# Each token block stored as two transfers of 64 rows, with the orders of all engines written anew

## The chip, the cores and the metric

One core of a Trainium2 chip. The time is that of one execution on the device, in microseconds (us); of several runs the median is taken.

## The reference

The kernel computes a linear attention with the delta rule and a two-layer network behind it. With 4 batches, 8 heads, 768 tokens and a head size of 48:

```python
for t in range(S):                       # per batch and head
    y[t] = q[t] @ state
    v_old = k_n[t] @ state               # k_n: k of unit length
    state += beta[t] * outer(k_n[t], v[t] - v_old)
x = y as [4*768 tokens, 8*48 = 384]
h = x @ w_in                             # 384 -> 2048
out = gelu_tanh(h) @ w_out               # 2048 -> 384, float32
```

## The kernel before

The tokens are cut into 12 chunks of 64 (`C`). A chunk holds the 64 tokens of all four batches and eight heads. The 128 partitions are two halves of 64 tokens: half 0 holds batches 0 and 1, half 1 batches 2 and 3. A *unit* u is a chunk (u // 2) with every other head (u % 2); there are 24.

*Preparation of a unit* (`prep`): POOL or another engine makes normalized k (`kn`), k times beta (`kb`) and q in bf16 (`qb`) in the tile `tok`. These are turned, so that the head size lies on the partitions, into `kT`: for units 0 to 5 by TensorE (`T`), from unit 6 on by a transposing transfer that SP issues (`turn.u`). TensorE then makes the products of keys (`G2`, `G`), which DVE masks (`ln`, `wp`). Five steps of two products each (`A`, `B`, line 620) build the inverse of a triangular matrix; DVE adds to the results (`rt`), ACT and DVE copy them (`bde`, `xi`), and POOL copies and selects (`bdc`, `X1`). The lengths of k are `sq`, `sum`, `pow`, `eps`, `inv`.

*The chain of a chunk* (`chain`): from the state, `K`, `R`, `Um`, `Un`, `S`, `Sn` make the next state, and `Q`, `O` and the copy `On` give the attention's output in the tile `xo`. It is turned into `xT` by another transposing transfer on SP (`turnx`, line 742) for all chunks but the first and the last.

*The network of a chunk* (`mlp`): 256 tokens. `up` (line 775, three matmuls) makes 128 columns of h from `xT`, ACT applies `gelu`, and `down` (line 787) sums over the 2048. The 256 tokens are two *blocks* of 128 rows, b = 0 and b = 1. A block is copied from PSUM into one of four buffers `ob` by ACT or DVE (`Z`, line 381) and stored (line 798). Block 0 holds 64 tokens of batch 0 in partitions 0 to 63 and 64 of batch 2 in the others; block 1 those of batches 3 and 1. Block 0 leaves in one transfer with two runs of 64 rows (`outw`, 192 KB, 12 in all), block 1 in two transfers of 64 rows (`out`, 96 KB each, 24 in all). All are issued by SP but one of the last block, which ACT issues. The names carry a number: chunk c has blocks 2c+4 and 2c+4.5, so the last are 26 and 26.5.

*The order.* No compiler orders the work. The table `ORDER` lists, for each engine, every operation in the order in which that engine runs it; SP's list holds the transfers (loads of q, k and v, the turns, the stores). For an operation of ACT, DVE or POOL the list also settles which engine runs it. `BANKS` lists the PSUM bank of each product. From both, `schedule` and `emit` work out which semaphores each operation waits for. An engine runs its list in order: what stands behind a waiting operation waits too. `fill` are matmuls without use (line 433), that keep TensorE at work at the start.

Of the kernel before, what the change touches and what calls it, by code (L numbers as in the profile page):

```python
# [12 lines left out]
C = 64  # L13
# [13 lines left out]
        Xh.0.8/1 B.2/1 B.3/0 T.4/0 A.2/2 up.3.5/0 A.3/1 up.3.5/1 B.2/2 up.3.5/2 B.3/1 up.3.5/3 up.3/0 fill/61 up.3/1 fill/62 up.3/2
        A.3/2 S.0.5/0 up.3.25/0 up.3/3 G2.4/0 G.4/0 B.3/2 up.3.25/1 A16.2/0 up.3.25/2 fill/63 up.3.25/3 fill/64 A16.3/0 K.2.5/0 B.2/3
        A.4/0 B.3/3 down.4.5/0 up.3.75/0 fill/65 up.3.75/1 B.4/0 up.3.75/2 A32.2/0 A32.3/0 up.3.75/3 down.4.54/0 A.4/1 B.3/4 B.2/4
        down.4.58/0 B.4/1 T.5/0 down.4.62/0 Um.2.5/0 Q.2.6/0 G2.5/0 G.5/0 A.4/2 O.2.7/0 fill/66 fill/67 B.4/2 S.2.5/0 down.4/0 A.5/0  # L30
        down.4.04/0 down.4.08/0 B.5/0 A16.4/0 down.4.12/0 B.4/3 A.5/1 up.5.25/0 up.5.75/0 up.5.25/1 B.5/1 up.5.25/2 A32.4/0 up.5.75/1
        up.5.25/3 A.5/2 up.5.75/2 B.4/4 up.5.75/3 up.5/0 B.5/2 up.5/1 K.4.5/0 G2.6/0 up.5/2 up.5/3 up.5.5/0 A16.5/0 up.5.5/1 G.6/0
        B.5/3 up.5.5/2 G2.7/0 up.5.5/3 A.6/0 A32.5/0 G.8/0 G2.8/0 B.6/0 down.6.5/0 B.5/4 A.6/1 down.6.54/0 down.6.58/0 G.7/0
        down.6.62/0 Um.4.5/0 A.8/0 B.6/1 Q.4.6/0 G2.9/0 O.4.7/0 down.6/0 A.6/2 B.8/0 G.9/0 down.6.04/0 B.6/2 A.7/0 down.6.08/0 A.9/0
        B.7/0 A.8/1 A16.6/0 down.6.12/0 B.9/0 B.8/1 A.7/1 B.6/3 up.7.25/0 A.9/1 up.7.25/1 up.7/0 up.7.25/2 B.7/1 A32.6/0 A.8/2 B.9/1
        up.7.25/3 B.6/4 up.7/1 S.4.5/0 up.7/2 A.7/2 up.7.75/0 up.7/3 up.7.5/0 B.8/2 up.7.5/1 B.7/2 up.7.5/2 K.6.5/0 up.7.75/1 up.7.5/3
        A16.7/0 up.7.75/2 A.9/2 up.7.75/3 B.7/3 A16.8/0 down.8/0 B.9/2 A32.7/0 down.8.04/0 B.8/3 B.7/4 down.8.08/0 A16.9/0 down.8.12/0
        Um.6.5/0 A32.8/0 Q.6.6/0 G2.10/0 O.6.7/0 S.6.5/0 G.10/0 B.8/4 down.8.5/0 B.9/3 down.8.54/0 A.10/0 G2.11/0 K.8.5/0 G.11/0
        down.8.58/0 B.10/0 down.8.62/0 up.9.75/0 up.9.75/1 up.9.25/0 up.9.75/2 A32.9/0 up.9.75/3 A.10/1 up.9.25/1 B.9/4 up.9.25/2
        up.9.5/0 up.9.25/3 up.9.5/1 B.10/1 up.9.5/2 A.11/0 up.9.5/3 G2.13/0 G.13/0 Um.8.5/0 B.11/0 A.10/2 Q.8.6/0 G2.12/0 O.8.7/0  # L40
        G.12/0 A.13/0 B.10/2 up.9/0 B.13/0 up.9/1 A.11/1 up.9/2 A.12/0 up.9/3 A.13/1 B.11/1 B.12/0 S.8.5/0 down.10/0 A.12/1
        down.10.04/0 A16.10/0 B.13/1 A.11/2 up.11.75/0 B.12/1 up.11.75/1 B.10/3 B.11/2 down.10.08/0 up.11.75/2 A.13/2 up.11.75/3
        A16.11/0 down.10.12/0 up.11/0 B.13/2 up.11/1 A.12/2 A32.10/0 B.11/3 up.11/2 up.11.25/0 B.12/2 up.11.25/1 up.11/3 up.11.25/2
        B.10/4 A16.12/0 up.11.25/3 A32.11/0 up.11.5/0 K.10.5/0 up.11.5/1 B.11/4 down.10.5/0 up.11.5/2 A16.13/0 B.12/3 up.11.5/3
        down.10.54/0 B.13/3 Um.10.5/0 down.10.58/0 A32.12/0 Q.10.6/0 S.10.5/0 O.10.7/0 G.14/0 down.10.62/0 down.12.5/0 A32.13/0 B.12/4
        down.12.54/0 B.13/4 down.12.58/0 G2.14/0 K.12.5/0 down.12/0 down.12.62/0 down.12.04/0 G2.15/0 G.15/0 A.14/0 Um.12.5/0
        down.12.08/0 B.14/0 down.12.12/0 Q.12.6/0 G2.17/0 O.12.7/0 G.17/0 up.13.75/0 up.13.5/0 up.13.75/1 up.13/0 up.13.75/2 up.13/1
        up.13.75/3 up.13/2 A.15/0 up.13/3 A.14/1 up.13.5/1 G2.16/0 B.15/0 up.13.5/2 up.13.25/0 B.14/1 up.13.5/3 up.13.25/1 G.16/0
        S.12.5/0 up.13.25/2 up.15.5/0 up.13.25/3 up.15.5/1 A.16/0 up.15.5/2 A.17/0 up.15.5/3 A.15/1 A.14/2 B.16/0 down.14/0 B.17/0
        down.14.04/0 B.14/2 B.15/1 A.16/1 up.15/0 down.14.08/0 A.17/1 B.16/1 up.15/1 A.15/2 up.15/2 down.14.12/0 B.15/2 up.15.25/0  # L50
        B.17/1 A16.14/0 up.15.25/1 A.16/2 up.15/3 up.15.25/2 A16.15/0 up.15.25/3 B.14/3 A.17/2 B.15/3 K.14.5/0 B.16/2 up.15.75/0
        B.17/2 up.15.75/1 A32.14/0 up.15.75/2 up.15.75/3 A32.15/0 G.18/0 G2.18/0 B.14/4 B.15/4 down.14.5/0 A16.17/0 down.14.54/0
        A16.16/0 down.14.58/0 Um.14.5/0 B.16/3 A.18/0 down.14.62/0 S.14.5/0 Q.14.6/0 G2.19/0 down.16/0 B.17/3 down.16.04/0 G.19/0
        O.14.7/0 K.16.5/0 down.16.08/0 A32.16/0 B.18/0 A.19/0 down.16.12/0 A32.17/0 down.16.5/0 B.19/0 down.16.54/0 B.16/4 A.18/1
        A.19/1 down.16.58/0 G2.20/0 G.20/0 down.16.62/0 B.17/4 up.17.5/0 B.18/1 up.17.5/1 up.17.75/0 B.19/1 A.20/0 Um.16.5/0
        up.17.75/1 up.17.5/2 G2.21/0 up.17.5/3 B.20/0 up.17.75/2 up.17.25/0 up.17.75/3 A.20/1 up.17.25/1 A.19/2 up.17.25/2 up.17/0
        up.17.25/3 Q.16.6/0 G.21/0 O.16.7/0 up.17/1 B.19/2 up.17/2 B.20/1 up.17/3 A.18/2 S.16.5/0 A.21/0 A16.19/0 B.18/2 down.18/0
        B.21/0 down.18.04/0 A16.18/0 down.18.08/0 B.19/3 A.21/1 A.20/2 B.18/3 K.18.5/0 down.18.12/0 up.19.5/0 B.21/1 up.19.5/1 B.20/2
# [797 lines left out]
```

## Time and profile before

| | |
|---|---|
| Median of 3 runs | 276.76 us (274.14 to 276.99) |
| The profiled execution | 277.13 us |
| its span, first to last instruction | 275.4 us |
| mean granted clock of TensorE in it | 0.986 |
| busy: PE, DVE, ACT, POOL | 250.3, 203.7, 176.6, 143.3 us |
| DMA: packets, bytes | 118348, 32.06 MB |

The page gives for each engine how long it was busy; PE is TensorE, PEld its weight loads, SP issues transfers. In 40 equal slices of the span (6.9 us each) a digit tells the busy share in tenths. `PEclk` is the clock granted to TensorE, and `DMA` the mean busy share of the 16 DMA engines. A row of the waits tells which engine stood at which line, and what ended that. The chain of waits goes back from the last instruction, at each step to what released it. `SPq` is the issue of a transfer by SP; "to landing" counts from there until the data have arrived.

### The profile page before, as it was taken

To read this page: it belongs to the slowest core of one execution; us is meant where nothing else is said; L and a number is where in the kernel's file an instruction comes from. 1 tells how busy PE (TensorE), PEld (TensorE's weight loads), DVE (VectorE), ACT (ScalarE), POOL (GpSimd) and SP (SyncE) were. 2 spreads that over 40 slices of the span, in tenths; PEclk is the share of its full clock that TensorE was granted. 3 is DMA by queue.
4 is the path that set the end of the run, shared out by engine and by line. 5 is a ranking of instruction groups with operands and counts; after the bars stand their busy time and mean duration, and the time that the engine had idled before them with its cause. 6 is when DMAs were issued, how large, how long until landed. Compare 5 with 4: busy or idle time off the path is not lost.

```text
span 275.4 us, 12507 instructions
## 1 busy us (share of the span) xinstructions
PE 250.3 (91%) x5640; PEld 190.0 (69%) x5652; DVE 203.7 (74%) x336; ACT 176.6 (64%) x273; POOL 143.3 (52%) x221
## 2 busy tenths in 40 slices
...
PEclk9999999999999999799999999999999999999996
DMA  7999999699999699857969669749077500321031
GB/s 118 160 159 142 159 201 203 119 152 134 162 150 144 98 155 130 163 114 162 156 105 154 68 135 137 163 89 151 7 150 80 126 14 2 68 65 45 0 69 45
DMA packets 118348, 32.06 MB, mean 116 GB/s; under 512 B 112408, under 2 KB 117528, under 8 KB 118296
## 3 DMA queue, kind: packets, MB, share of 16 engines
...
q14 instruction: 8, 0.07, 0.1%
...
## 4 chain that ended last, share of the span: by engine, by line
PE 65%; DMA 16%; DVE 6%; POOL 3%; ACT 3%; issue 2%; SPq 1%; ACTq 0%; POOLq 0%; DVEq 0%
PE ps L787 19%; PE ps L775 18%; PE ps L620 14%; DMA kT<-tok 6%; DMA xT<-xo 5%; DMA qraw<-in_q_dram 3%; PE ps L433 2%; PE ps L592 2%; PE ps L665 2%; PE ps L544 1%; DMA braw<-in_beta_dram 1%; PE ps L552 1%; DVE wp L574 1%; PE ps L524 1%; PE ps L698 1%
## 5 line engine op out<-in xcount | busy, mean ns | idle before, releaser
L775 PE MATMUL ps<-xT,W 128*128 128x256 bf16 x576 | 84.3, 276 | 5.5 <-DMA xT<-xo 5.3
L381 ACT ACTIVATE bd<-ps 64x512 bf16<-64x512 f32 x114 | 66.5, 590 | 18.3 <-PE ps L620 16.3
L787 PE MATMUL ps<-W,gT 128*128 128x384 bf16 x384 | 75.6, 326 | 0.0
L780 ACT ACTIVATE gT<-ps 128x1024 bf16<-128x1024 f32 x48 | 48.4, 1020 | 31.5 <-PE ps L775 31.0
L775 PEld LDWEIGHTS ps<-xT,W 128*128 128x128 bf16 x576 | 49.1, 99 | 14.3 <-issue 5.4
L627 DVE TENSOR_TENSOR rt<-ps,two 128x512 bf16<-128x512 f32 x66 | 44.3, 686 | 11.3 <-PE ps L620 10.7
L614 POOL COPY bd<-xi 64x256 f32<-64x256 f32 x64 | 25.1, 395 | 40.6 <-ACT xi L381 28.3
L610 POOL TENSOR_SCALAR_AFFINE_SELECT bd<-ln 64x512 bf16<-64x512 bf16 x44 | 28.8, 656 | 29.5 <-DVE ln L559 25.5
L787 PEld LDWEIGHTS ps<-W,gT 128*128 128x128 bf16 x384 | 32.7, 97 | 15.9 <-ACT gT L780 0.2
L381 DVE CAST bd<-ps 64x512 bf16<-64x512 f32 x42 | 28.8, 687 | 5.4 <-PE ps L620 4.6
L627 DVE TENSOR_TENSOR rl<-ps,two 128x384 bf16<-128x384 f32 (+1 forms) x44 | 21.0, 484 | 11.3 <-PE ps L620 10.8
L574 DVE CAST_PREDICATED wp<-mup,ps 128x1024 bf16<-128x1024 uint16 x22 | 26.7, 1218 | 2.9 <-PE ps L544 2.8
L493 POOL TENSOR_TENSOR nrm<-nrm,half 128x16 f32<-128x16 f32 x9 | 26.7, 2965 | 0.2
L620 PE MATMUL ps<-rt,bd 128*128 128x64 bf16 x528 | 26.0, 193 | 0.6 <-DVE ln L559 0.5
L620 PE MATMUL ps<-wp,bd 128*128 128x64 bf16 (+1 forms) x528 | 24.8, 188 | 1.6 <-ACT bd L381 1.0
L620 PEld LDWEIGHTS ps<-rt,bd 128*128 128x128 bf16 x528 | 21.8, 98 | 5.3 <-DVE rt L627 1.7
L620 PEld LDWEIGHTS ps<-wp,bd 128*128 128x128 bf16 x528 | 21.1, 97 | 5.5 <-ACT bd L381 1.2
L381 ACT ACTIVATE xi<-ps 128x512 bf16<-128x512 f32 (+1 forms) x35 | 17.6, 516 | 10.2 <-PE ps L592 4.9
L516 POOL TENSOR_TENSOR tok<-tok,bsb 128x384 bf16<-128x384 bf16 x21 | 17.3, 831 | 10.8 <-PE ps L707 6.6
L514 POOL TENSOR_TENSOR tok<-kraw,nrm 128x384 bf16<-128x384 f32 x22 | 18.2, 833 | 6.5 <-DVE nrm L497 6.1
L559 DVE CAST_PREDICATED ln<-mlo,ps 128x512 bf16<-128x512 uint16 (+1 forms) x26 | 16.6, 643 | 4.5 <-PE ps L552 4.1
L433 PE MATMUL ps<-wz 128*128 128x512 bf16 x56 | 16.9, 418 | 2.1 <-DVE wz L387 1.2
...
## 6 DMA issues: line engine op xcount, KB each, us to landing
...
out_dram<-ob SPq DMA_DIRECT2D x23, 96.0 KB, 3.8
...
kraw<-in_k_dram SPq DMA_DIRECT2D x3, 96.0 KB, 3.6
```

The source lines that it names most:

```text
L381: return e.activation(out, in_, ACT.Copy) if e is nc.scalar else e.tensor_copy(out, in_)
L433: return e.matmul(P(f"fill{i}")[:, :], wz[:, 0:128], wz[:, 0:512])
L493: e.tensor_tensor(nr[:, 1, hx], nr[:, 0, hx], half[:, hx], ALU.pow),
L514: A("dve" if u < 2 else POOL, z + "kn", lambda e, P: e.tensor_tensor(kn, kr, nr[:, 3, hx].rearrange("t (p g) -> t p g", p=2).unsqueeze(3). ...
L574: A("dve", z + "wp", lambda e, P: e.copy_predicated(wp[s][:, :, :], mup[:, :].bitcast(U16).unsqueeze(1).to_broadcast([128, H, 2 * C]), P(p ...
L610: A("pool", z + "X1", lambda e, P, src=src, dst=dst: e.affine_select(out=dst, in_=src, compare_op=ALU.not_equal, fill=1.0, base=0, pattern ...
L614: A("pool", z + "bdc", lambda e, P, src=src, dst=dst: e.tensor_copy(dst.bitcast(F32), src.bitcast(F32)), reads=[w("xi")], writes=[n(f"bd{a ...
L620: ins = e.matmul(P(name)[:, C * h + lo:C * h + C], bd[s][:, h, :], rhs[:, h, lo:C])
L627: A("dve", z + f"rt{lo or str()}", lambda e, P, i=i, lo=lo, r_=r_: e.tensor_tensor(r_[:, :, lo:C], P(ps(f"A{i}")).rearrange("p (h t) -> p ...
L775: ins = e.matmul(P(ph)[:, w * f:w * f + w].rearrange("p (x t) -> p x t", x=2), W1[:, j, 128 * (i + f):128 * (i + f) + 128], x_[:, :, j, :] ...
L780: A("act", z + "gelu", lambda e, P, i=i, ph=ph: e.activation(g_[:, i:i + nf, 0:w], P(ph).rearrange("p (f t) -> p f t", f=nf), ACT.Gelu_app ...
L787: ins = e.matmul(P(po)[:, 0:DM], g_[:, f, 128 * b:128 * b + 128], W2[:, f, :], start=(f == 0), stop=(f == FC - 1))
```

## The change

In `mlp`, every block is stored in two transfers of 64 rows; the case of one transfer with two runs is gone. There are 48 transfers out instead of 36, of the same bytes. The lists of all five engines and the banks are written anew; of that part the diff shows one line.

```diff
-        loadk.-40/0 beta.-24.5/0 loadk.-40/3 loadk.-40/2 loadk.-39/0 loadk.-39/1 loadq.-40/1 loadq.-39/0 loadq.-40/0 loadq.-39/1
+        loadk.-40/1 beta.-24.5/1 beta.-24.5/0 loadk.-40/3 loadk.-39/0 loadk.-39/1 loadq.-39/1 loadq.-39/0 loadq.-40/0 loadq.-40/1
...
-                rows = out.rearrange("(a p c t) m -> p c a t m", a=2, p=2, t=C)[b % 2, g[b // 2]]
-                for a in (0, 1) if b % 2 else (slice(0, 2),):
-                    A("act" if final and a else "sp", z + "out" if b % 2 else z + "outw", lambda e, P, a=a, o_=o_, rows=rows, b=b: e.dma_start(
-                        rows[a ^ 1] if b % 2 else rows, o_[hf(a), :] if b % 2 else o_[:, :]),
+                for a in range(2):
+                    r0 = (2 * (a ^ b % 2) + b % 2) * S + C * g[b // 2]
+                    A("act" if final and a else "sp", z + "out", lambda e, P, a=a, r0=r0, o_=o_: e.dma_start(out[r0:r0 + C, :], o_[hf(a), :]),
                       reads=[f"ob{oi}"], dma=f"o{oi}" if not final else f"of{a}", pos=kz)
```

The order of the large pieces on PE (units, chains, ups and downs) is nearly the same; between them products change places, and there are 61 fillers instead of 68. On ACT and DVE, 29 of the copies `bde` go each way, 11 copies `xi` go from ACT to DVE and 7 back. Of the squares `sq`, four go from ACT to POOL and one comes back.

SP, around the turns of units 10 and 11 (`kT4`, `kT5`) and the turn of `xT` behind them (`xT3`, of chunk 3). `s0` to `s3` are the semaphores of PE, ACT, DVE and POOL. Before:

```order
L462 DMA kraw0<-in_k_dram 64x16x48
L798 DMA out_0_dram<-ob0 2x64x384
L462 DMA qraw0<-in_q_dram 64x16x48
L798 DMA out_0_dram<-ob2 2x64x384 [waits s2]
L527 DMA_TRANSPOSE kT4<-tok0 128x12x128 [waits s3]
L527 DMA_TRANSPOSE kT5<-tok0 128x12x128 [waits s3]
L462 DMA kraw1<-in_k_dram 64x16x48 x2
L462 DMA vraw2<-in_v_dram 64x16x48
L742 DMA_TRANSPOSE xT3<-xo1 128x6x128 [waits s1]
```

In the change:

```order
L797 DMA out_0_dram<-ob0 64x384 x2
L461 DMA qraw1<-in_q_dram 64x16x48
L461 DMA kraw0<-in_k_dram 64x16x48 x2
L461 DMA qraw2<-in_q_dram 64x16x48 [waits s3]
L526 DMA_TRANSPOSE kT4<-tok0 128x12x128 [waits s3]
L526 DMA_TRANSPOSE kT5<-tok0 128x12x128 [waits s3]
L797 DMA out_0_dram<-ob1 64x384
L461 DMA vraw2<-in_v_dram 64x16x48
L461 DMA vraw1<-in_v_dram 64x16x48
L461 DMA kraw1<-in_k_dram 64x16x48 [waits s3]
L741 DMA_TRANSPOSE xT3<-xo1 128x6x128 [waits s1]
```

Of the two stores with two runs ahead of the turns, one is now two halves; the other block (6) leaves later, and the wait for DVE in front of the turns is gone. A wait for POOL stands there now, for a load of q. Between the turns and that of `xT` stand one half store and three loads, where there were three loads.

SP, the end of its list, from the copy of block 24 (`ob0`) on. Before:

```order
L798 DMA out_0_dram<-ob2 2x64x384
L798 DMA out_0_dram<-ob0 2x64x384 [waits s1]
L798 DMA out_0_dram<-ob1 64x384 [waits s2]
L798 DMA out_0_dram<-ob1 64x384
L798 DMA out_0_dram<-ob3 64x384 [waits s1]
L798 DMA out_0_dram<-ob2 2x64x384 [waits s2]
```

In the change:

```order
L797 DMA out_0_dram<-ob0 64x384 [waits s1]
L797 DMA out_0_dram<-ob0 64x384
L797 DMA out_0_dram<-ob2 64x384 x2
L797 DMA out_0_dram<-ob3 64x384
L797 DMA out_0_dram<-ob1 64x384 x2
L797 DMA out_0_dram<-ob3 64x384 [waits s1]
L797 DMA out_0_dram<-ob2 64x384 [waits s2]
L797 DMA out_0_dram<-ob2 64x384
```

The last block (`ob2`, block 26) was one transfer with two runs and is now two halves, both issued by SP. Block 22 (`ob2`, too) and a half of 22.5 (`ob3`) now leave behind block 24.

ACT, around the output of the first chunk (`xo0`), ahead of the first gelu. Before:

```order
L381 ACTIVATE us0<-ps 128x384
L381 ACTIVATE xo0<-ps 128x8x48
L488 ACTIVATE sq0<-kraw1 128x768
L381 ACTIVATE xo0<-ps 128x8x48
L381 ACTIVATE xT0<-ps 128x384
L381 ACTIVATE bd2<-ps 64x8x64
```

In the change:

```order
L487 ACTIVATE sq0<-kraw1 128x768
L380 ACTIVATE us0<-ps 128x384
L380 ACTIVATE xo0<-ps 128x8x48 x2
L380 ACTIVATE xT0<-ps 128x384
L380 ACTIVATE bd3<-ps 64x8x64 x2
L380 ACTIVATE bd2<-ps 64x8x64
L809 ACT_TABLE_LOAD
```

The square of k has moved from between the two halves of `xo` to ahead of both. The load of gelu's table, which stood some ten operations earlier (line 811 before), now stands behind these copies.

More of the change, by code (lines that the diff above doesn't have):

```diff
@@ L27 @@
[L27 to L58, printed above, removed]
@@ L92 @@
-        gelu.19.75/0 bde.20/4 bde.20/5 bde.22/0 bde.22/1 bde.21/4 bde.21/5 bde.23/0 xi.22/0 gelu.21.5/0 gelu.21.75/0 bde.22/2
-        gelu.21/0 Un.20.5/0 gelu.21.25/0 xi.23/1 xi.22/1 bde.23/4 bde.22/5 Z.22.5/0 gelu.23.25/0 gelu.23/0 gelu.23.5/0 gelu.23.75/0
-        gelu.25.75/0 gelu.25/0 gelu.25.25/0 gelu.25.5/0 Z.24/0 Z.26.5/0 out.26.5/1
+        loadk.-40/0 tabS.-30/0 tmpl.-11/0 loadk.-40/2 tri.-7/0 ladj16.-0.2/0 triw.1/0 pow.0/0 triw.-7/0 tri.-9/0 tri.-5/0 sqh.1/0
+        pow.1/0 kTh.0/0 triw.-1/0 ladj16.1.8/0 sq.-140/0 kTh.1/0 pow.-140/0 xih.0/0 qb.2.01/0 xih.0/1 qb.0.01/0 qb.1.01/0 xih.1/1
@@ L95 @@
+        bde.20/5 bde.23/0 xi.22/0 gelu.21.5/0 gelu.21.75/0 xi.23/0 gelu.21.25/0 gelu.21/0 Un.20.5/0 bde.23/3 bde.22/3 bde.23/2
+        Z.20.5/0 bde.23/4 bde.22/5 gelu.23/0 gelu.23.25/0 gelu.23.5/0 gelu.23.75/0 Z.24.5/0 Z.24/0 gelu.25/0 gelu.25.25/0 gelu.25.5/0
+        gelu.25.75/0 Z.26.5/0 out.26.5/1
     """,
     "dve": """
-        wz.-200/0 pad.-9/0 one.-40/0 bdz.3/0 bdz.6/0 bdz.2/0 identf.-29/0 sqh.0/0 sumh.0/0 tri.-5/0 eps.0/0 inv.0/0 kn.0/0 betaN.-28/1
-        betaN.-28/0 sumh.1/0 triw.-5/0 eps.1/0 ladj16.0.8/0 inv.1/0 kTh.0/0 kn.1/0 lnh.0/1 lnh.0/0 wphh.0/0 X1h.0/0 wphh.0/1
@@ L119 @@
-        rt16.22/0 Z.20.5/0 R.22.5/0 rt32.23/0 Z.22/0 rt32.22/0 bde.23/5 bde.22/4 Un.22.5/0 On.22.7/0 xT.22.8/0 Z.24.5/0 Z.26/0
+        wz.-200/0 one.-40/0 bdz.6/0 pad.-9/0 ladj32.-0.2/0 ladj32.2.8/0 identf.-29/0 sqh.0/0 ladj32.1.8/0 sumh.0/0 eps.0/0 inv.0/0
+        kn.0/0 betaN.-28/0 betaN.-28/1 kb.0/0 sumh.1/0 eps.1/0 inv.1/0 kn.1/0 lnh.0/0 wphh.0/0 wphh.0/1 lnh.0/1 sum.-140/0 rth.0/0
+        eps.-140/0 ladj16.0.8/0 lnh.1/0 rth.0/1 lnh.1/1 inv.-140/0 X1h.1/1 wphh.1/1 wphh.1/0 rth.1/1 rth.1/0 rth.0/3 rth.0/2 triw.-5/0
@@ L120 @@
+        On.22.7/0 xT.22.8/0 Z.26/0
     """,
     "pool": """
[L122 to L125 removed]
@@ L134 @@
-        kb.20/0 bdc.16/2 bdc.16/3 X1.19/1 bdc.17/3 X1.19/0 bdc.17/2 kb.21/0 X1.20/1 X1.20/0 bdc.18/0 kn.22/0 bdc.19/0 bdc.19/1 X1.21/1
-        qb.23.01/0 X1.21/0 bdc.18/1 qb.22.01/0 kb.22/0 kb.23/0 bdc.20/1 bdc.20/0 bdc.19/2 bdc.18/2 bdc.18/3 bdc.21/0 bdc.21/1 bdc.19/3
-        bdc.21/3 bdc.21/2 bdc.20/3 bdc.20/2 X1.22/1 X1.22/0 X1.23/1 X1.23/0 bdc.22/0 bdc.22/1 bdc.23/0 bdc.23/1 bdc.23/2 bdc.23/3
-        bdc.22/2 bdc.22/3
+        half.-28/0 ident.-29/0 masks.-12/2 masks.-12/0 two.-12/0 ident2.-29/0 mup.-12/0 two.-12/1 tmplz.-11/0 mup.-12/1 triw.-3/0
@@ L145 @@
-        loadk.16/1 loadv.6/1 turnx.6.8/0 loadq.10/1 out.4.5/0 out.4.5/1 turn.13/0 turn.12/0 out.8.5/1 loadq.12/0 loadv.8/1 outw.8/0
-        turnx.8.8/0 loadq.10/0 out.6.5/0 out.8.5/0 loadq.14/1 out.6.5/1 loadq.12/1 loadk.18/0 loadv.6/0 turn.14/0 loadq.14/0
-        loadk.18/1 turn.15/0 loadv.8/0 turn.17/0 turnx.10.8/0 loadv.12/1 turn.16/0 outw.12/0 out.10.5/0 turnx.12.8/0 outw.10/0
-        out.12.5/0 loadv.10/0 loadv.10/1 loadv.12/0 loadq.16/0 loadq.16/1 turn.18/0 turn.19/0 out.12.5/1 loadv.14/0 out.10.5/1
@@ new lines @@
+        loadv.-38/0 loadk.-37/0 loadk.-37/1 loadv.-38/1 loadk.2/1 loadv.-36/0 loadk.2/0 loadv.-36/1 loadk.4/1 loadq.-37/1 loadq.-37/0
+        loadq.2/0 loadk.4/0 loadq.2/1 loadk.6/1 loadk.8/1 loadk.6/0 loadk.8/0 loadk.10/0 turn.6/0 loadk.10/1 loadq.4/0 turnx.2.8/0
+        loadq.4/1 out.4.5/1 loadv.0/0 loadv.0/1 turn.7/0 turn.8/0 loadv.4/0 turn.9/0 loadq.6/0 loadq.6/1 loadk.12/0 loadk.12/1
+        loadv.2/0 out.6.5/1 loadq.8/0 turnx.4.8/0 loadv.2/1 loadq.8/1 out.4/0 out.4/1 loadq.10/0 loadk.14/0 loadk.14/1 loadq.12/0
@@ new lines @@
+        turn.10/0 turn.11/0 out.4.5/0 loadv.6/1 loadv.4/1 loadk.16/1 turnx.6.8/0 loadq.12/1 out.8/0 out.6.5/0 turn.13/0 turn.12/0
+        out.8.5/0 loadk.16/0 loadv.6/0 loadq.10/1 turnx.8.8/0 loadq.14/0 out.6/0 out.6/1 loadq.14/1 loadk.18/1 loadq.18/0 loadv.8/1
+        turn.15/0 turn.14/0 out.8/1 loadk.18/0 loadv.8/0 out.10/0 out.8.5/1 turn.17/0 turnx.10.8/0 loadq.18/1 turn.16/0 turnx.12.8/0
+        loadv.10/1 out.10/1 out.12.5/0 loadv.14/0 out.10.5/0 out.10.5/1 out.12.5/1 loadv.10/0 turn.18/0 loadq.16/1 loadq.16/0 out.12/0
```

184 lines of the change are left out of this document (106 added, 78 removed), and 17 rows, old and new, of the table BANKS.

## The prediction

> **What bounds the kernel now.** I read the page first, then the busy time in four stretches, then the chain of waits and the waits of PE and SP, and last the places where PE stands.
>
> ```profile
> span 275.4 us, 12507 instructions
> PEclk9999999999999999799999999999999999999996
> DMA  7999999699999699857969669749077500321031
> 0.00:60.00 60.00, 52.57 (x1205) 36.05 (x1218) 52.83 (x110) 42.52 (x77) 37.45 (x59) 1.00 1.06 157
> 60.00:220.00 160.00, 151.74 (x3689) 119.44 (x3687) 129.19 (x195) 111.34 (x168) 101.72 (x154) 0.99 0.85 128
> 220.00:266.00 46.00, 45.99 (x755) 34.48 (x751) 21.18 (x31) 22.74 (x30) 4.16 (x10) 1.00 0.15 33
> 266.00:275.40 9.40, 0.00 (x0) 0.00 (x0) 0.56 (x1) 0.00 (x0) 0.00 (x0) 0.77 0.28 75
> ```
>
> In a row of a stretch stand its bounds, its length, then the busy time of PE, of the weight loads, DVE, ACT and POOL, the clock, the DMA share and GB/s. PE, the TensorE, is the bound: 250.3 us of the 275.4 are matmuls. So a microsecond can be won only where PE stands: 7.4 us before 60 us (the start), 8.3 us between 60 and 220 us, nothing from 220 to 266 us, and 9.4 us behind the last matmul. In the last two of these, as the next rows show, PE stands for transfers.
>
> **The tail.** The last matmul ends at 266.0 us. Then comes one copy, one store, and a wait.
>
> ```profile
> 266.03 0.56 DVE L381 COPY ob<-ps 128x384 f32<-128x384 f32 x1 [7.51 <-PE ps L787]
> 265.96 1.20 SPq L798 DMA_DIRECT2D out_dram<-ob  x2
> SPq L304 <- DMA out_dram<-ob: 7.7, 1, 7.7
> 270.00:274.00 4.00, 0.00 (x0) 0.00 (x0) 0.00 (x0) 0.00 (x0) 0.00 (x0) 0.65 0.13 45
> out_dram<-ob SPq DMA_DIRECT2D x23, 96.0 KB, 3.8
> out_dram<-ob ACTq DMA_DIRECT2D x1, 96.0 KB, 4.5
> DMA to landing us min/median/max: 2.1/4.0/7.0
> L798 SPq DMA_DIRECT2D out_dram<-ob x35: 467/589/2173, 88.7 to 266.6; - x35
> ```
>
> The store of the last block is issued by 267.16 us and SP waits 7.7 us for it, to 274.9 us. Meanwhile the DMA share is 0.13 of sixteen engines, which is two engines: the one transfer of 2x64 rows is moved by two of them. At 45 GB/s its 192 KB need 4.4 us alone. The transfers of 64 rows that the kernel has already land 3.8 us (SP) or 4.5 us (ACT) after issue.
>
> **The middle.** A transfer that sits on two engines for so long also stands in front of what is issued behind it.
>
> ```profile
> 90.37 2.17 SPq L798 DMA_DIRECT2D out_dram<-ob x1
> 92.59 9.25 DMA kT<-tok
> 104.33 6.78 DMA xT<-xo
> 111.24 2.72 PE L775 MATMUL ps<-xT,W 128*128 128x256 bf16 x12 [3.09 <-DMA xT<-xo]
> 93.00:97.00 4.00, 4.00 (x98) 3.27 (x95) 3.89 (x7) 3.70 (x7) 2.89 (x5) 1.00 0.21 60
> 100.00:120.00 20.00, 15.82 (x442) 11.98 (x441) 13.30 (x21) 8.78 (x13) 12.12 (x20) 0.91 0.96 161
> 111.20:114.20 3.00, 2.96 (x22) 2.19 (x23) 0.00 (x0) 0.00 (x0) 1.40 (x3) 0.51 1.01 186
> kT<-tok SPq DMA_TRANSPOSE x18, 4.8
> xT<-xo SPq DMA_TRANSPOSE x10, 4.1
> 151.53 0.57 SPq L798
> 152.73 7.96 DMA xT<-xo
> 160.82 1.14 PE L775 MATMUL ps<-xT,W 128*128 128x256 bf16 x9 [1.73 <-DMA xT<-xo]
> 216.73 0.31 PE L665 MATMUL ps<-st,kT 48*64 48x48 bf16 x16 [1.10 <-issue]
> ```
>
> Two such stores were issued at 88.75 and 90.37 us. The turn of unit 10 issued behind them lands after 9.25 us, where the median is 4.8, and from 93 to 97 us the DMA engines are busy to 0.21, a fifth, with loads and turns waiting. The chain of waits runs through this turn to the turn of xT at 104.33 us (6.78 us) and to PE, which waits 3.09 us for it. Then the granted clock is 0.51 for 3 us: twelve matmuls of L775 take 2.72 us. In all, PE stands 4.18 us between 100 and 120 us. The same at 151.53 us: one such store, then a turn of xT that lands after 7.96 us instead of 4.1, and PE stands 1.73 us. At 216.7 us PE stands 1.10 us for nothing that the profile shows.
>
> **The change, part by part.** All twelve transfers of two runs become pairs of 64 rows; every order is new. I make the sum against the profiled execution, 277.1 us (span 275.4).
>
> (1) Tail. The copy stays. The first half is issued by 267.16 us as now; the second starts then, takes 0.59 us to issue and lands 3.8 us after its start: 271.0 us, against 274.9. That is -3.9 us. With a landing of 4.5 us it is -3.2, with the shortest of any store, 2.1 us, it is -5.6. In the new order SP issues seven more halves shortly before, from the copy of block 24 on. After the matmuls of that block PE has ten groups of up and eight of down left:
>
> ```profile
> 114.78 0.33 PE ps L775 x3
> 259.49 0.65 PE ps L787 x4
> ```
>
> 10 x 0.33 + 8 x 0.65 = 8.5 us. The fifth of the seven frees the buffer of the last block but one: 0.56 (copy) + 5 x 0.59 + 3.8 = 7.3 us, against the 7.9 us at which it is written. It fits, with 0.6 us to spare; if it doesn't, the excess comes on top.
>
> (2) The stand around 108 us. It costs 4.18 us of idle PE and the slow clock: twelve matmuls of L775 take 1.31 us at full clock (four times the 0.33 us for three). So 2.72 - 1.31 = 1.4 us more, 5.6 in all. With the turn of unit 10 at the median it lands 4.45 us earlier, and the DMA engines have four more microseconds for the loads. But in the new order three loads and a half store still stand between the turn of unit 11 and that of xT for chain 3, so some of the 6.78 us stays. I take -4.0; bounds 0 and -5.6.
>
> (3) The stand at 159 us: no store stands ahead of that turn in the new order. At 4.1 us it would land 3.9 us earlier, more than the 1.73 us that PE waits. I take -1.3; bounds 0 and -1.7.
>
> (4) The stand at 216 us.
>
> ```profile
> 207.38 5.07 SPq L527 DMA_TRANSPOSE kT<-tok x1
> ```
>
> SP needs 5.07 us to issue one turn just before, behind a store of two runs, but the row of the stand names no releaser. I take -0.4; bounds 0 and -1.1.
>
> (5) The new PE order has seven fillers fewer. Behind the first up stand three now, where seven stood between matmuls that had their data:
>
> ```profile
> 43.45 0.22 PE ps L433
> 48.22 0.21 PE ps L433
> ```
>
> 4 x 0.21 = 0.8 us is what I take; bounds 0 and 7 x 0.21 = 1.5 us, because the other three may have filled gaps that stay.
>
> (6) ACT at the start.
>
> ```profile
> 35.90 0.84 ACT L488 ACTIVATE sq<-kraw 128x768 f32<-128x768 f32 x1
> 27.47 1.28 ACT L811 ACT_TABLE_LOAD   x1
> 59.29 1.46 ACT sq L488 x2
> 58.28 1.45 POOL L610 TENSOR_SCALAR_AFFINE_SELECT bd<-ln 64x512 bf16<-64x512 bf16 x2 [6.31 <-DVE ln L559]
> ```
>
> The square that stood between the two halves of xo moves ahead of them (the chain of waits passes through it), two squares (1.46 us, also on the chain) go to POOL, which stands 6.31 us just there; without this idle time they would cost POOL 2 x 1.46 = 2.9 us. The table load moves from ahead of xi to ahead of kT of unit 4 and the first gelu; if that were late, it costs 1.3 us. I take -0.7; bounds -2.0 and +1.5.
>
> (7) What the new order makes late. Twelve more issues are 12 x 0.59 = 7.1 us of SP. Most lie in SP's own waits:
>
> ```profile
> SPq L742 <- ACT bd L381: 26.0, 7, 9.2
> SPq L798 <- ACT ob L381: 22.7, 4, 15.1
> ```
>
> From 84 to 113 us SP issues almost without a pause, and there two of the new stores (1.2 us) push turns and loads back. Stores that wait for a copy of ACT or DVE now stand ahead of the turns of units 19, 21 and 23, so a late copy holds these. No row prices that; the nearest is what PE waits for turns of xT now, three waits that sum to 5.3 us. I take +2.0; bounds 0 and +5.
>
> Sum: -3.9 - 4.0 - 1.3 - 0.4 - 0.8 - 0.7 + 2.0 = **-9.1 us**, so 277.1 becomes 268.0. The median of the three runs is 276.76, 0.4 us lower; **267.7 us** is the forecast for it.
>
> The Trainium skill (DMA: Bandwidth & Descriptors, section Rules for kernel authors) speaks against the change: two transfers to disjoint partition halves are not worth it, use one of 128 partitions, because both halves spread over the same sixteen engines. By that, term (1) would be +0.6 us for the second issue and terms (2) and (3) would be nothing. The row of 0.13 disagrees with its premise here: the one transfer is on two engines. The same page (section Why a DMA increments its semaphore by 16 and not by 1) has it that the engines used are the largest number up to 16 that divides the outermost sizes, which for 2x64 rows is 2: the trace agrees, with 0.13.
>
> **The rivals.** *Only the tail is won.* The stands move to other places: PE has nothing to spare, and the DMA share is 1.06 in the first 60 us and 0.96 from 100 to 120 us, so the loads may make turns late without wide stores too. Then (1) and half of (5) and (6) hold, -3.9 - 0.75, and half of (7), since the stands that stay are not counted twice, +1.0: 273.1 on the median's scale. Against it: the share of 0.21 at 93 us is engine time that comes back.
>
> *Nothing is won by halves.* Two halves land as late as one whole, because what takes the time is the write and not the two engines: the tail +0.6, the middle as before, (5) and (6) -1.5: 275.9. Against it: 64 rows land in 3.8 us now, in the same program.
>
> *SP becomes the bound, and it is slower.* SP issues in order. If all of the 7.1 us of new issues delayed turns for which PE stands, with the tail's -3.9 and nothing from the middle, it is +3.2: 280.0. This decides as soon as SP has no wait left between 60 and 220 us; the 26.0 and 22.7 us above say that it has.
>
> *All is won.* The full bounds of (1) to (4), -14.0, and (5) at -1.5, with no new wait: 261.3.
>
> **How the numbers follow.** Forecast 0.56, only the tail 0.22, nothing by halves 0.08, SP the bound 0.07, all won 0.07. The range of 8 in 10 is 261.5 to 275.0: it leaves out the slower rival, most of the one by halves, half of all won and a little of the tail's. A measurement of this kernel tells a change of over 1%, 2.8 us, from none; faster by that is below 274.0. Forecast, all won and most of the tail's case (0.16 of 0.22) are there: 0.79. Slower: 0.07. The rest, 0.14, is within 1%.
>
> **What would show it.** Right: no 4 us stretch at a share of 0.13 behind the last matmul, and SP's last wait at about 3.3 us instead of 7.7; turns of kT and xT that land at most 7 us after issue; no PE wait of 3 us for xT and a clock of 1.00 between 100 and 120 us; PE idle between 60 and 220 us at 2 to 5 us. (1) is wrong if SP's last wait stays above 6 us; (2) and (3) if PE's waits for xT still sum to 5 us; (5) and (6) if the last matmul of the first 60 us' work (the first down) does not come earlier. The forecast falls if PE is idle over 9 us between 60 and 220 us.

## The result and the profile after

| | before | after |
|---|---|---|
| Median | 275.9 us (4 runs, 274.14 to 276.99) | 268.12 us (4 runs, 266.42 to 270.48) |
| The profiled execution | 277.13 us | 267.68 us |
| its span | 275.4 us | 265.6 us |

The ratio of the times is 0.9703, with a 95% interval of 0.9615 to 0.9791. It is taken from fast runs alone, so the run of 270.48 us, in a slower state of the chip, is not in it. A second measurement of the changed kernel, told below, gave 264.56 us and 0.9609 (0.9559 to 0.9659). The change makes the kernel 3 to 4% faster; the forecast was 267.7 us.

The page of the changed kernel, to be laid beside that of before (the lines of the code are one lower now: matmuls of up 774, of down 786, stores 797):

```profile
span 265.6 us, 12514 instructions
PEclk9999999999999999799999999999999999999999
DMA  5998999969999999975996568537528631040042
```

Its busy time in four stretches, with the columns that the prediction explains:

```profile
0.00:60.00 60.00, 53.73 (x1201) 34.67 (x1202) 49.84 (x104) 43.55 (x78) 41.28 (x62) 1.00 1.03 155
60.00:220.00 160.00, 156.89 (x3798) 123.28 (x3797) 138.06 (x208) 107.81 (x165) 104.32 (x157) 0.99 0.79 130
220.00:258.00 38.00, 38.00 (x631) 29.17 (x631) 16.50 (x25) 18.67 (x25) 3.17 (x8) 1.00 0.18 38
258.00:265.60 7.60, 3.67 (x23) 1.99 (x21) 0.56 (x1) 1.59 (x3) 0.00 (x0) 0.92 0.32 78
```

PE was idle 7.4 us before 60 us, 8.3 us from 60 to 220 and 9.4 us behind the last matmul. Now it is idle 60.00 - 53.73 = 6.3, 160.00 - 156.89 = 3.1 and 7.60 - 3.67 = 3.9 us. The three differences are -1.2, -5.2 and -5.5 us; PE's busy time is 2.0 us more, and together that is the span's -9.8 us.

The first difference is not shown to be a gain. The 2.0 us are fillers, 18.9 us of them in place of 16.9, because the profile before has no record of some. Its row of the fillers' weight loads, its row of their matmuls, and the row of the matmuls in the changed kernel:

```profile
L433 PEld LDWEIGHTS ps<-wz x68: 95/98/147, 1.2 to 58.4; 128*128 128x128 bf16 x68
L433 PE MATMUL ps<-wz 128*128 128x512 bf16 x56 | 16.9, 418 | 2.1 <-DVE wz L387 1.2
L432 PE MATMUL ps<-wz 128*128 128x512 bf16 x61 | 18.9, 417 | 1.2 <-DVE one L392 1.2
```

Of 68 fillers 12 lack their matmul, so a part of the 7.4 us that the prediction read as idle was work. In a run below that keeps the old orders, the one with only the last transfer in halves, all 68 are recorded, and PE is idle 60.00 - 55.24 = 4.8 us before 60 us:

```profile
0.00:60.00 60.00, 55.24 (x1222) 36.36 (x1223) 52.26 (x111) 42.84 (x77) 37.54 (x59) 1.00 1.07 158
```

Nor does the first down come earlier. It starts (the first of the two times) at 49.7 us before and at 51.1 us now:

```profile
L787 PE MATMUL ps<-W,gT x384: 322/326/337, 49.7 to 265.7; 128*128 128x384 bf16 x192
L786 PE MATMUL ps<-W,gT x384: 322/326/527, 51.1 to 261.3; 128*128 128x384 bf16 x192
```

The last matmul ends at 261.67 us where it ended at 266.0, and the tail is 3.9 us where it was 9.4. The gain lies where the forecast put it: in the tail and in the middle.

The tail, first in the timeline (start, length, what, and the idle time before it):

```profile
261.78 0.56 DVE L380 COPY ob<-ps 128x384 f32<-128x384 f32 x1 [13.53 <-PE ps L786]
262.36 1.11 SPq L797 DMA_DIRECT2D out_dram<-ob  x2
```

Then in SP's waits (sum, times, longest):

```profile
SPq L303 <- DMA out_dram<-ob: 1.6, 1, 1.6
```

Then the busy time behind the last copy:

```profile
262.80:265.20 2.40, 0.00 (x0) 0.00 (x0) 0.00 (x0) 0.00 (x0) 0.00 (x0) 0.82 0.61 156
```

And the stores in the part on transfers, with the median to landing:

```profile
out_dram<-ob SPq DMA_DIRECT2D x47, 96.0 KB, 2.8
DMA to landing us min/median/max: 2.1/2.8/4.8
```

The same for the four halves of the last two blocks:

```profile
DMA to landing us min/median/max: 2.1/2.2/2.4
```

SP waits 1.6 us at the end where it waited 7.7. Behind the last copy the DMA share is 0.61, where it was 0.13. All halves land after 2.8 us in the median and 4.8 at most; before, halves took 3.8.

The middle, from the groups (busy time, mean of one, idle time before them):

```profile
L774 PE MATMUL ps<-xT,W 128*128 128x256 bf16 x576 | 83.1, 273 | 0.2
```

The turns, with the median to landing, and then the extremes for kT:

```profile
xT<-xo SPq DMA_TRANSPOSE x10, 3.8
kT<-tok SPq DMA_TRANSPOSE x18, 5.0
DMA to landing us min/median/max: 3.7/5.0/7.6
```

The 7.6 us are those of the turn of unit 10, which took 9.25 before; in the second profile of the changed kernel it takes 5.0.

Two stretches around the stand that is left:

```profile
100.00:120.00 20.00, 18.00 (x526) 14.03 (x522) 14.99 (x23) 10.36 (x16) 13.76 (x23) 0.91 0.95 142
107.30:109.00 1.70, 1.70 (x59) 1.48 (x60) 1.32 (x2) 0.16 (x1) 0.66 (x1) 0.51 0.91 213
```

And the stand in the timeline:

```profile
107.22 0.21 PE L551 MATMUL ps<-kT 48*64 48x64 bf16 x1 [1.93 <-issue]
```

The matmuls of up no longer wait for turns of xT: 0.2 us of idle time stands before them, and it was 5.3 us for these turns alone. One stand is left at 105 to 107 us. It is of another kind: the row names issue, not a transfer, and half a clock follows it, as it followed the stand of before.

### The profile page after: what moved, and what is told of

It reads as the page before. It is cut to its first block, busy times and chain, and to the rows that moved or that the text cites. A ratio compares the mean times of both kernels' runs of the same rounds, so it can differ in the third digit from the quotient of the medians.

```text
span 265.6 us, 12514 instructions
## 1 busy us (share of the span) xinstructions
PE 252.3 (95%) x5645; PEld 189.1 (71%) x5645; DVE 205.0 (77%) x336; ACT 171.6 (65%) x268; POOL 148.8 (56%) x226
## 4 chain that ended last, share of the span: by engine, by line
PE 80%; DVE 9%; DMA 3%; POOL 3%; issue 3%; ACT 1%; ACTq 0%; POOLq 0%; DVEq 0%
PE ps L786 23%; PE ps L774 22%; PE ps L619 17%; PE ps L432 3%; DMA W<-in_moe_w_in_dram 3%; PE ps L664 3%; PE ps L551 2%; PE ps L591 2%; PE ps L543 2%; PE ps L697 1%; DVE bd L380 1%; PE ps L523 1%; PE ps L706 1%; DVE ln L558 1%; DVE rt L626 1%
## 5 line engine op out<-in xcount | busy, mean ns | idle before, releaser
L380 ACT ACTIVATE bd<-ps 64x512 bf16<-64x512 f32 x114 | 65.7, 588 | 33.7 <-PE ps L619 32.1
L774 PE MATMUL ps<-xT,W 128*128 128x256 bf16 x576 | 83.1, 273 | 0.2
L774 PEld LDWEIGHTS ps<-xT,W 128*128 128x128 bf16 x576 | 48.4, 98 | 8.4 <-DMA W<-in_moe_w_in_dram 0.4
L380 ACT ACTIVATE xi<-ps 128x512 bf16<-128x512 f32 (+1 forms) x34 | 16.3, 494 | 9.5 <-PE ps L591 6.5
L432 PE MATMUL ps<-wz 128*128 128x512 bf16 x61 | 18.9, 417 | 1.2 <-DVE one L392 1.2
```

The lines of the kernel that those rows point to most:

```text
L380: return e.activation(out, in_, ACT.Copy) if e is nc.scalar else e.tensor_copy(out, in_)
L432: return e.matmul(P(f"fill{i}")[:, :], wz[:, 0:128], wz[:, 0:512])
L774: ins = e.matmul(P(ph)[:, w * f:w * f + w].rearrange("p (x t) -> p x t", x=2), W1[:, j, 128 * (i + f):128 * (i + f) + 128], x_[:, :, j, :] ...
```

## The experiments

All times are medians; each set was measured beside the kernel before on the same chip: 275.4 us for the first four runs, 276.28 for the next four, 275.23 for the last four. The theory is that the whole gain is that of the halves, because two runs of 64 rows put a transfer on two DMA engines, and that the new orders bring nothing. The rivals are that the new orders bring part of it, and that what helps is the smaller transfer, not the engines.

**The new orders without the halves.** In the changed kernel block 0 is stored in one transfer again; `outw` stands in SP's list where the first half stood.

```diff
-                for a in range(2):
-                    A(..., z + "out", ... e.dma_start(out[r0:r0 + C, :], o_[hf(a), :]),
+                rows = out.rearrange("(a p c t) m -> p c a t m", a=2, p=2, t=C)[b % 2, g[b // 2]]
+                for a in (0, 1) if b % 2 else (slice(0, 2),):
+                    A(..., z + "out" if b % 2 else z + "outw", ... e.dma_start(rows[a ^ 1] if b % 2 else rows, ...),
```

> The new orders of all engines, but block 0 of each chunk stored in one transfer of two runs again, at the place of the first of its two halves in SP's list. Theory A (the transfers of two runs, which two DMA engines move, hold up the tail and the turns behind them): the tail behind the last matmul is 9 to 10 us again instead of 3.9, turns land after 7 to 10 us, PE stands 6 to 9 us between 60 us and the last 46 us instead of 3.1; 274 to 277 us. Theory B (the middle was won by the new orders, only the tail by the halves): the tail is back, PE still stands about 3 us in the middle; 272 to 274 us.

Measured: 280.06 us, ratio 1.0192 (1.0135 to 1.0248), above the 274 to 277 us of theory A. The orders alone lose 4.7 us. Its middle, with 6.35 us of idle PE, and its longest wait of PE for a turn:

```profile
60.00:220.00 160.00, 153.65 (x3712) 121.51 (x3713) 134.51 (x203) 105.16 (x159) 103.21 (x156) 0.98 0.84 127
PE ps L550 <- DMA kT<-tok: 3.0, 1, 3.0
```

Its tail in the timeline:

```profile
256.81 12.41 SPq L796 DMA_DIRECT2D out_dram<-ob  x7
259.95 4.71 PE L785 MATMUL ps<-W,gT 128*128 128x384 bf16 x28
267.40 0.56 DVE L379 COPY ob<-ps 128x384 f32<-128x384 f32 x1 [16.16 <-DMA out_dram<-ob]
267.65 0.49 ACT L379 ACTIVATE ob<-ps 128x384 f32<-128x384 f32 x1 [5.56 <-DMA out_dram<-ob]
```

The last matmul ends at 264.66 us, the span is 276.0: a tail of 11.3 us. The last two copies start 2.7 and 3.0 us after it, because they wait for a store to leave the buffer `ob`. The new list puts the wide stores of blocks 24 and 22 directly behind each other, from 256.81 us on, and that of block 26 follows at the end. This execution took 278.04 us and is the fastest of the six, so it shows only a part of the 4.7 us; where the rest lies is open.

**The halves without the new orders.** In the kernel before each `outw.n/0` is replaced in place, and the code of the store is that of the change.

```diff
-        loadv.4/1 turnx.4.8/0 loadv.2/1 loadq.8/1 loadk.14/1 loadk.14/0 outw.4/0 loadq.8/0 outw.6/0 ...
+        loadv.4/1 turnx.4.8/0 loadv.2/1 loadq.8/1 loadk.14/1 loadk.14/0 out.4/0 out.4/1 loadq.8/0 out.6/0 out.6/1 ...
```

> The orders of before, with each transfer of two runs replaced, at its place, by its two halves. Theory A: tail 4 to 5 us, PE stands 2 to 4 us between 60 and 220 us instead of 8.3, no wait of PE for xT over 1 us; 266 to 269 us, as the whole change. Theory B: the tail alone is won, PE still stands about 8 us in the middle; 270 to 271.5 us. Rival C (twelve more issues of 0.6 us make SP late in an order that was not made for them): 272 us or more, with PE waiting for turns.

Measured: 266.87 us, ratio 0.9651 (0.9591 to 0.9711): -8.5 us. That is the whole gain of the change in its first measurement. PE is idle 5.0 us in the middle, a little more than theory A's 2 to 4:

```profile
60.00:220.00 160.00, 154.99 (x3800) 122.24 (x3797) 132.83 (x201) 115.46 (x175) 102.28 (x155) 1.00 0.89 128
```

**Only the last transfer in halves**, and **all but the last** (in the kernel before; SP's list has the halves in place of each `outw` that is cut in two):

```diff
+                wide = b % 2 == 0 and gi < len(GROUPS) - 1     # all but the last: gi == len(GROUPS) - 1
+                for a in (slice(0, 2),) if wide else (0, 1):
```

> The kernel before with the last block alone stored in two halves. Theories A and B both: only the tail changes, from 9.4 us to 4 to 5 us, so 270.5 to 272 us; the stands of PE in the middle stay at 7 to 9 us. If the halves land no earlier than the one transfer, 276 us.

> The kernel before with all blocks in halves but the last, which stays one transfer of two runs. Theory A: tail 8 to 9.4 us, PE stands 2 to 4 us between 60 and 220 us instead of 8.3; 270.5 to 272.5 us, and the gains of this and of the last block alone add up to that of both. Theory B: no gain, 275 to 277 us.

Measured: 271.76 us, ratio 0.9858 (0.9817 to 0.9899), and 270.07 us, ratio 0.9778 (0.9732 to 0.9824). The parts are -3.6 and -5.3 us; their sum, -8.9, is what both together give (-8.5). The busy time in the middle, with only the last one in halves:

```profile
60.00:220.00 160.00, 153.69 (x3766) 121.48 (x3765) 130.60 (x197) 112.97 (x170) 102.61 (x155) 0.99 0.93 128
```

The same with all but the last in halves, and there also behind the last copy:

```profile
60.00:220.00 160.00, 155.68 (x3818) 123.11 (x3816) 133.84 (x202) 116.78 (x176) 103.00 (x156) 1.00 0.87 130
264.00:268.00 4.00, 0.00 (x0) 0.00 (x0) 0.00 (x0) 0.00 (x0) 0.00 (x0) 0.50 0.11 37
```

With only the last one in halves PE is idle 6.3 us in the middle, where 7 to 9 were expected; with all others in halves, 4.3 us, where 2 to 4 were. The last transfer of two runs again leaves its stretch at a share of 0.11 there. With only the last one in halves the stand of the prediction's term (4), named issue, is there as before:

```profile
214.28 0.31 PE L664 MATMUL ps<-st,kT 48*64 48x48 bf16 x16 [1.20 <-issue]
```

**One transfer of 128 rows that lie together.** Orders of before; only where block 0 goes is changed.

```diff
-                rows = out.rearrange("(a p c t) m -> p c a t m", a=2, p=2, t=C)[b % 2, g[b // 2]]
+                    r0 = ... if b % 2 else 2 * (g[0] % 2) * S + C * (g[0] - g[0] % 2)
-                        rows[a ^ 1] if b % 2 else rows, o_[hf(a), :] if b % 2 else o_[:, :]),
+                        out[r0:r0 + C, :] if b % 2 else out[r0:r0 + 2 * C, :], o_[hf(a), :] if b % 2 else o_[:, :]),
```

> The orders of the kernel before, block 0 of a group still in one transfer of 128 rows, but to 128 neighbouring rows of the output in place of two runs of 64; so block 0 lands at other rows of the output, everything else is as before. Theory (the cost of the wide transfer is that its two runs put it on two of the sixteen DMA engines; one transfer or two does not matter): it lands in 2.5 to 4 us, DMA share over 0.5 behind the last matmul, no turn above 7 us for it, tail 4 to 5 us, time as with two halves in the old order, 264 to 269 us. Rival (the size of one transfer is what holds others up, 192 KB in one piece; halves help because they are two): landing near 6 us, 272 to 277 us.

Measured: 265.01 us, ratio 0.9621 (0.9572 to 0.9669). From the part on transfers:

```profile
out_dram<-ob SPq DMA_DIRECT2D x12, 192.0 KB, 2.8
out_dram<-ob SPq DMA_DIRECT2D x23, 96.0 KB, 3.0
```

Its stretches, in the middle and behind the last copy:

```profile
60.00:220.00 160.00, 156.47 (x3861) 123.94 (x3860) 134.83 (x203) 116.97 (x176) 102.52 (x156) 1.00 0.82 128
258.80:261.20 2.40, 0.00 (x0) 0.00 (x0) 0.02 (x1) 0.00 (x0) 0.00 (x0) 0.81 0.57 164
```

The transfer of 192 KB lands after 2.8 us, as fast as one of 96 KB, and the share behind the last copy is 0.57. With the same number of transfers as before, the same bytes and the old orders, the time is that of the halves. The rival of the smaller transfer falls.

**Four runs of 32 rows in place of two of 64** (the diff is the one above, with the destination in four interleaved runs):

```diff
+                        ... else out[r0:r0 + 2 * C, :].rearrange("(t y) m -> y t m", y=4), ...
```

> The orders of the kernel before, block 0 in one transfer of 128 rows whose rows in the output are written as four interleaved runs of 32, within 128 neighbouring rows; so the rows of block 0 land elsewhere in the output. Theory (engines used = runs of the outer size): four engines, landing about half of that with two runs (6.4 to 7 us where it is alone), 3.5 to 5 us, tail 5.5 to 7 us, DMA share about 0.25 behind the last matmul, time between halves and before: 268 to 273 us. Rival (any transfer with an interleaved form is as slow as the one with two runs): 274 to 277 us and share 0.13.

Measured: 267.22 us, ratio 0.9701 (0.9648 to 0.9753), a little better than expected. Of its profiled execution (270.88 us) only the tail is read, here a stretch behind the last copy:

```profile
266.00:267.00 1.00, 0.00 (x0) 0.00 (x0) 0.00 (x0) 0.00 (x0) 0.00 (x0) 0.58 0.24 75
```

The share is 0.24, which is four engines of sixteen. The last matmul ends at 263.05 us and the span is 269.1: a tail of 6.05 us, between 3.5 (128 rows together: 258.16 to 261.7) and 9.4 (two runs). The tail is 2.5 us longer than in the run before this one, and the time is 2.2 us longer. By these two numbers four engines cost in the tail, and hardly in the middle.

**Halves that are each on two engines.** Both halves of block 0 write their 64 rows as two interleaved runs of 32; otherwise as the halves in the old orders.

```diff
-                ... e.dma_start(out[r0:r0 + C, :], o_[hf(a), :]),
+                ... e.dma_start(out[r0:r0 + C, :] if b % 2 else out[r0:r0 + C, :].rearrange("(t y) m -> y t m", y=2), o_[hf(a), :]),
```

> The orders of the kernel before, block 0 in two transfers of 64 rows, but each writes its rows as two interleaved runs of 32 within its 64 rows of the output (the rows of block 0 come out in another order). Theory (two engines are the cost, the number of transfers is not): although in halves, each of them lands after about 3.5 to 7 us on its two engines, the two behind each other, the stretch behind the last matmul has a share near 0.13 again, tail 8 to 10 us, 273 to 280 us. Rival (halving is the gain whatever their form): 264 to 269 us.

Measured: 276.01 us, ratio 0.9993 (0.9951 to 1.0035). A wait of PE:

```profile
PE ps L775 <- DMA xT<-xo: 2.1, 1, 2.1
```

The stretches:

```profile
60.00:220.00 160.00, 152.76 (x3711) 120.29 (x3712) 130.01 (x196) 112.25 (x169) 102.91 (x155) 0.99 0.90 128
270.00:272.00 2.00, 0.00 (x0) 0.00 (x0) 0.00 (x0) 0.00 (x0) 0.00 (x0) 0.50 0.13 44
```

The stores:

```profile
out_dram<-ob SPq DMA_DIRECT2D x47, 96.0 KB, 3.9
```

Everything is back: the share of 0.13 behind the last copy, a wait for xT, 7.2 us of idle PE in the middle, and a tail from 264.63 to 274.5, 9.9 us. Halves that are on two engines are worth nothing. With the run of 128 rows together this settles the cause from both sides: one transfer on sixteen engines has the gain, and halves on two engines have not. The middle varies from one execution to the next, but these two groups stay apart in it. Where block 0 leaves on two engines (before, the new orders without the halves, only the last one in halves, and this run) PE is idle 6.3 to 8.3 us between 60 and 220 us; in the nine other profiles, without that of the four runs, it is 2.4 to 5.0 us.

**The last half issued by ACT.** Old orders with halves; `out.26/1` moves from the end of SP's list to the end of ACT's:

```diff
-        ... Z.24/0 Z.26.5/0 out.26.5/1
+        ... Z.24/0 Z.26.5/0 out.26.5/1 out.26/1
-        ... out.24.5/1 out.26.5/0 out.26/0 out.26/1
+        ... out.24.5/1 out.26.5/0 out.26/0
```

> Orders of the kernel before with every block in two halves, and the second half of the very last block issued by ACT in place of SP, beside the first. Theory: SP issued the two halves 0.5 to 0.6 us apart at the end, ACT is idle there, so the tail shrinks by 0.3 to 0.6 us against SP alone: span 264.0, time 266.0 to 266.8 us where all halves in the old order gave 266.9. Rival (the landing decides, not the issue): no difference, 266.5 to 267.3.

Measured: 266.32 us, ratio 0.9681 (0.9631 to 0.9731), against 0.9651 with SP alone. The tail is 3.76 us (261.34 to 265.1) against 3.99; no difference that can be told.

**The changed kernel once more, and the old orders with halves once more**, side by side:

> The changed kernel once more, on the same chip and beside the next one, to compare the two sets of orders directly. Theory (the whole gain is the halves; the new orders give nothing): ratio to the kernel before 0.965 to 0.978, that is 266 to 270 us, and not below the old orders with halves. Rival (the new orders bring the 0.5 to 1 us of the forecast's terms 5 and 6): at least 1 us below the old orders with halves.

> The old orders with all blocks in two halves, once more, beside the changed kernel. Theory: 265.5 to 268 us, at or up to 1.5 us below the changed kernel. Rival (the new orders help): 1 us or more above the changed kernel.

Measured: 264.56 us, ratio 0.9609 (0.9559 to 0.9659), and 265.89 us, ratio 0.9657 (0.9607 to 0.9706). The changed kernel is 1.3 us below the old orders here, and was 1.2 us above them in the first measurements (268.12 and 266.87 us). Side by side the rival's 1 us is met and the theory missed, but the intervals overlap in both comparisons and the signs differ, so neither is shown. What can be said is that the orders change less than about 1% with halves. In this execution of the changed kernel the clock was full from 100 to 120 us:

```profile
100.00:120.00 20.00, 18.35 (x561) 14.70 (x556) 17.25 (x25) 12.42 (x18) 15.14 (x25) 1.00 0.96 142
```

The stand named issue was shorter:

```profile
106.49 0.21 PE L551 MATMUL ps<-kT 48*64 48x64 bf16 x1 [1.31 <-issue]
```

**Without the late fillers.** Old orders with halves, less `fill/61` to `fill/67` in PE's list, and their entries in `BANKS`. The first of them:

```diff
-        ... up.3.5/3 up.3/0 fill/61 up.3/1 fill/62 up.3/2
+        ... up.3.5/3 up.3/0 up.3/1 up.3/2
```

> The old orders with halves, less the seven fillers between 70 and 95 us that the changed kernel lacks too. Theory of the forecast's term 5 (each filler of 0.2 to 0.4 us stands on PE's path there): 0.5 to 1.5 us less than with them, 265.0 to 266.5 us. Rival (they fill stretches in which PE would wait for other engines, and what follows waits anyway): within 0.4 us of the run with them.

Measured: 264.18 us, ratio 0.9612 (0.9556 to 0.9668), where it is 0.9657 with them: 1.2 us less by the ratios and by the spans (262.2 and 263.4), 1.7 by the medians. The intervals overlap. Nor do the fillers stand between 70 and 95 us: in the profile before, their weight loads lie between 42.6 and 58.4 us, and four of the seven stand ahead of the first down in the list. It starts at 49.6 us with them and at 49.7 without:

```profile
L787 PE MATMUL ps<-W,gT x384: 322/326/337, 49.6 to 259.0; 128*128 128x384 bf16 x192
L786 PE MATMUL ps<-W,gT x384: 322/326/337, 49.7 to 258.0; 128*128 128x384 bf16 x192
```

These four cost nothing that shows. The size of the difference is what the forecast's term asks for, but it is not shown to come from the fillers.

**One transfer to the right rows, on sixteen engines.** Old orders. ACT writes the tokens of the two batches in turn, so that the transfer's outer size becomes 64.

```diff
-   ... e.activation(g_[:, i:i + nf, 0:w], P(ph).rearrange("p (f t) -> p f t", f=nf), ACT.Gelu_apprx_tanh)
+   ... e.activation(g_[:, i:i + nf, 0:w].rearrange("p f (b t a) -> p (f b) a t", b=2, a=2), P(ph).rearrange("p (x a t) -> p x a t", a=2, t=C), ACT.Gelu_apprx_tanh)
-                rows = out.rearrange("(a p c t) m -> p c a t m", a=2, p=2, t=C)[b % 2, g[b // 2]]
+                rows = out.rearrange("(a p c t) m -> p c a t m" if b % 2 else "(a p c t) m -> p c t a m", a=2, p=2, t=C)[b % 2, g[b // 2]]
-                        rows[a ^ 1] if b % 2 else rows, o_[hf(a), :] if b % 2 else o_[:, :]),
+                        rows[a ^ 1] if b % 2 else rows, o_[a::2, :] if b % 2 else o_[:, :]),
```

> The old orders, block 0 again in one transfer, to its right rows: the activation writes the tokens of the two batches in turn (column 2t+a), so that row 2t+a of the tile belongs to batch a and the transfer's outer size is 64 in place of 2; the halves of block 1 take every second partition. Theory (only the outer size of 2 was bad): block 0 lands in 2.5 to 4 us, tail 3.5 to 5 us, 264 to 267 us, at or below all halves, with 12 issues fewer on SP. Rival (writing every second column makes ACT slower, or taking every second partition makes the halves slower): gelu above its 1.02 us by 10% or more, or landings above 4 us, 268 to 275 us.

Measured: 268.97 us, ratio 0.9767 (0.9722 to 0.9813): 3.1 us above the halves. Its chain, by engine:

```profile
PE 73%; ACT 15%; DMA 4%; DVE 3%; issue 3%; DVEq 0%; ACTq 0%
```

Its gelu in the groups:

```profile
L780 ACT ACTIVATE gT<-ps 128x1024 bf16<-128x1024 f32 x48 | 62.3, 1321 | 22.0 <-PE ps L775 21.4
```

Its stores:

```profile
out_dram<-ob SPq DMA_DIRECT2D x12, 192.0 KB, 2.9
out_dram<-ob SPq DMA_DIRECT2D x23, 96.0 KB, 2.6
```

The chain of the halves in the old orders, beside it:

```profile
PE 84%; DVE 6%; DMA 4%; issue 3%; ACT 2%; SPq 0%; DVEq 0%; ACTq 0%
```

And their gelu:

```profile
L780 ACT ACTIVATE gT<-ps 128x1024 bf16<-128x1024 f32 x48 | 48.4, 1020 | 25.3 <-PE ps L775 24.9
```

The transfers do what the theory says: 2.9 us for the wide one, 2.6 for every second partition, a tail of 3.5 us (265.87 to 269.4). But a gelu takes 1.32 us in place of 1.02, 48 x 0.30 = 14 us more of ACT, and ACT's share of the chain goes from 2 to 15%. The rival was right about the price, and the time lies in its range. No version tried beats the changed kernel by more than can be told.

## Why the prediction was right

- **The tail, (1): right, in the direction of its bound.** Forecast -3.9 us, which leaves a tail of 5.5; the last transfer alone in halves gives -3.6, with a tail of 5.4 us (263.55 to 268.9). The page of the changed kernel shows more, -5.5, since the half was taken to land in 3.8 us. That median is of a kernel in which halves stand behind transfers on two engines; without these the median is 2.8, the last four land after 2.1 to 2.4, and the wait of SP is 1.6 us and not 3.3.
- **The middle, (2) to (4): right in kind, somewhat too large in size.** Forecast -5.7. All but the last in halves give -5.3 us, but about 1.5 us of that is tail: 7.9 us (260.36 to 268.3) in place of 9.4. Adding them to the halved last transfer gives 271.76 - 266.87 = 4.9 us. So by the times the middle is worth 4 to 5 us; by the idle time of PE it is about 3 (7.0 us on average in the four profiles with two engines, 3.8 in the nine without). PE's waits for xT went from 5.3 us to nearly none, as (2) and (3) said. But with only the last one in halves they are 0.2 us as well, and PE waits 1.5 us for turns of kT there, so the two terms can't be priced one by one. Term (4), put at -0.4 us with a bound of -1.1, has evidence: its stand is in all three profiles of the old orders with two engines (1.10 us before, 1.20 with only the last one in halves, 0.50 with halves on two engines), and in every other profile PE has no wait between 200 and 220 us. The new orders with two engines have none there either, and why such transfers bring the stand about, no run shows.
- **Two signs failed** in the profile of the changed kernel and held in its second one: a full clock between 100 and 120 us (0.91, then 1.00), and turns that land within 7 us (7.6 at most, then 6.8). The stand that goes with the slow clock is not one for xT.
- **The orders, (5) to (7): right only as a sum.** Forecast +0.5 us, measured +1.2 and -1.3. Of the parts, (5) and (6) were wrong by their own sign, a first down that comes earlier; it comes 1.4 us later. The new list has four more groups of up ahead of it, 4 x 0.33 = 1.3 us, and four fillers fewer, so the sign is a weak one; but a gain at the start is shown nowhere. (7) stands for something real that hardly shows: with transfers of two runs the new orders cost 4.7 us, and with halves nothing that can be told. With the halves the kernel is less sensitive to the order; the forecast had treated the two as independent terms.
- **The number was partly luck.** The first median, 268.12 us, is 0.4 us from the forecast, the second, 264.56, is 3.1 below it. In the profile the tail gave 1.6 us more than its term, the middle by its idle time 0.5 less, and the start nothing that shows where 1.5 us were put down; these and the +2.0 of (7) cancel in part.
- **The rivals.** Only the tail: that would be 273.1 us, and the middle's gain is there, so it falls. SP the bound: 24 issues in place of 12 cost nothing that can be told (266.87 us with 24 in the old orders, 265.01 with 12 of 128 rows together). Nothing by halves: it falls for this form of transfer, and holds once the transfer has another form. The Trainium skill (DMA: Bandwidth & Descriptors, Rules for kernel authors) advises one transfer of 128 partitions rather than two halves. For 128 rows that lie together the runs agree: 265.01 us with one, 266.87 and 265.89 with two. For two runs of 64 they do not: 275 us with one. What decides is the page's other rule (Why a DMA increments its semaphore by 16 and not by 1), that the engines used are the largest number up to 16 that divides the outermost sizes; the shares agree at 0.13 for an outer size of 2 and 0.24 for 4.
